# Decode attention: scores of a whole head over 512 keys on 64 partitions, K turned in place in halves

## The chip, the core and the metric

The kernel runs on one core of one Trainium2 chip. The metric is the device time of one launch in microseconds, lower is better. Engines: PE (matmul), DVE (vector), ACT (scalar), POOL (GpSimd, only used for a few memsets), SP (issues every DMA).

## What is computed

Four layers act on one token `x` of width 640: attention (A), mixer (B), A, B, both times with the same weights and caches. Each A takes 32 heads of width 192 over the last 4096 keys of the caches:

```python
W = min(4096, max(256, Sk // 4))                      # 4096
q = (x @ wq).reshape(B, Sq, Hq, Dh)                   # 32 heads x 192
k = k_cache[:, :, Sk - W:, :]; v = v_cache[:, :, Sk - W:, :]
scores = jnp.einsum("bhqd,bhkd->bhqk", q, k) * (Dh ** -0.5)
p = _softmax(scores, axis=-1)
o = jnp.einsum("bhqk,bhkd->bhqd", p, v)
return o.transpose(...).reshape(B, Sq, Hq * Dh) @ wo
```

The mixer B is a small chain of layer norms, a gelu and two matrices (640x1536 and 1536x640); it is not touched here. K and V of one head are 1.5 MB each in bf16, so nearly all the work is reading the caches: 32 heads, K and V, twice.

## The kernel before

**Cells.** SBUF holds 12 cells of 128 x 6144 bf16 (`NCELL`), each big enough for K or V of one head (partition p has keys 32p to 32p+31). `take` (L146) gets the cell that was freed longest ago, `give` (L152) frees one. `layer_stream` (L247) fixes the order of all loads: in each group of four heads it alternates K of the next group with V of the running one, then wo. `need` (L291) issues the loads in this order, and SP issues each as soon as the last reader of its cell is done. At most eight loads are under way: each waits for the landing of the eighth before it.

**Kept heads.** Layer 0 takes the groups from the last to the first, layer 1 from the first to the last. K of heads 0 to 7 (`NKEEP`), which are the last two groups of layer 0 and the first two of layer 1, stay in SBUF in turned form and aren't read again in layer 1. V of head 3, and V of head 2 and a part of V of head 4 in several places, stay as well. At the end of layer 0 the kept K hold eight cells, and four go round for the last loads: V 4 to 7 make room for V 0 to 3, two blocks of wo, w3 and w4.

**Turning K.** TensorE needs K with the head's width on partitions. `transpose_quart` (L433) has DVE turn blocks of 32x32 words, a quarter of a head per instruction (128x768 uint32, L450). A kept head's quarters go into a cell of their own (`take(("T", h))`). All others go through the four quarters of one cell, the area (`area`, L430). K's cell is freed when its last quarter is turned (`give(("k", layer, h))`, L452).

**Scores.** `scores` (L524) multiplies the query blocks (16 columns of weights, `Qblk`) with turned K. Each quarter of K has its own 32 partitions of PSUM, that is its own column group of the array: six matmuls of 256 keys per quarter, 24 per head. A call with two quarters alternates between two column groups, a call with four (kept heads in layer 1) between four. The scores of four heads gather on 128 partitions x 256 in one half of `ST_both`, one PSUM bank; `next_scores` (L544) takes the halves in turn.

**Softmax of a group.** `softmax_steps` (L551) returns seven steps: `part_max` (DVE, maximum per partition, L557), `turn_max` (PE, L562), `full_max` (DVE, L567 and L572), `spread_max` (PE, L580; ACT copies the bias, L583, and does exp with its sum, L586), `turn_p` (DVE, L591 and L593), `swap` (PE, 16 matmuls, L605; ACT, L608; PE sums, L613) and `recip` (DVE, L620 and L622).

**The order.** It is written out by hand in `attention` (L726), and each engine does its instructions in this order. `T(h, half)` turns two quarters, `S(h, half, ...)` scores them. For each group the loop at L819 first does the softmax of the running group around `T` and `S` of the next group's first head (L857 to L897), together with the query projection and the output projection of the group before. Then, for each running head, come PV (`pv`, L645: 16 matmuls of PT and V, L654, then DVE drains O with L661), `T` and `S` of the next group's next head, and `o_fold` (L663) of the running one. In layer 1 the first half of the next K is turned ahead of PV's drain (L913). The last group but one (`hurry`) scores its last two heads after PV of its second and third head (L941 to L953), and starts the last softmax there. In layer 1 that group has an order of its own (`quick`).

Of the kernel before, what the change touches and what calls it, by code (L numbers as in the profile page):

```python
# [18 lines left out]
P = 128  # L19
# [40 lines left out]
def kernel(  # L60
# [31 lines left out]
    NT = 4  # L92
    QUART = NFB * (NGK // NT) * P * 2
    FREE = NT * QUART
# [57 lines left out]
    def give(key):  # L152
        free.append(cell_of.pop(key))
# [276 lines left out]
    area = [None, 0]  # L430
    SW = P * NGK // NT

    def transpose_quart(layer, h, q):  # L433

        if layer == 1 and h < NKEEP:
            return kept[h][:, q * QUART:(q + 1) * QUART]
        Kn = need("k", layer, h)
        NY = NFB * (NGK // NT)
        Ku = Kn[:].bitcast(U32).rearrange("p (j y b) -> p j y b", j=NJ4, b=32)
        if layer == 0 and h < NKEEP:  # L440
            if q == 0:
                kept[h] = take(("T", h))
            T = kept[h][:, q * QUART:(q + 1) * QUART]
        else:
            if area[0] is None:
                area[0] = take(("area", layer))
            T = area[0][:, area[1] * QUART:(area[1] + 1) * QUART]
            area[1] = (area[1] + 1) % NT
        Tu = T.bitcast(U32).rearrange("p (y j b) -> p j y b", y=NY, j=NJ4)
        nc.vector.transpose(Tu, Ku[:, :, q * NY:(q + 1) * NY])  # L450
        if q == NT - 1:
            give(("k", layer, h))  # L452
        return T

    def qproj_steps(c, xc, part=None, row=None):
# [29 lines left out]
        def spread():  # L485
# [7 lines left out]
            Xq = o_bytes[:, 2 * (SW + 2 * QH):][:, 0:4 * n].rearrange("p (t b) -> p t b", b=4)  # L493
# [30 lines left out]
    def scores(h, Ts, q0, ST_ps, hq):  # L524
# [3 lines left out]
        views = [T.rearrange("p (g f i t) -> p g f i t", f=NFB, g=ng, i=P) for T in Ts]  # L528
        for f in range(NFB):
            for t in range(2):  # L530
                n = 2 * f + t
                for i, T4 in enumerate(views):
                    r = 32 * (q0 + i)
                    nc.tensor.matmul(  # L534
                        ST_ps[r:r + QW, :].rearrange("p (g i) -> p g i", g=ng), lhsT=Q[n],
                        rhs=T4[:, :, f, :, t],
# [3 lines left out]
    ST_both = psS.tile([P, 2 * SW], F32, name="ST_ps")  # L540
# [3 lines left out]
    def next_scores():  # L544
        turn[0] += 1
        i = turn[0] % 2
        return ST_both[:, i * SW:(i + 1) * SW]
# [3 lines left out]
    def softmax_steps(n, ST_ps, sc, space, bank=None):  # L551
        held = {}
        halves = space.bitcast(BF16)

        def part_max():
            pm = short("pm")
            nc.vector.tensor_reduce(out=pm[:], in_=ST_ps, op=ALU.max, axis=AX.X)  # L557
# [560 lines left out]
```

## Time and profile before

| | |
|---|---|
| median of 3 runs | 511.87 us (511.39 to 512.92) |
| the profiled execution | 511.54 us, of which the span is 509.7 us |
| busy: PE, DVE, ACT, POOL | 313.2, 292.6, 48.9, 3.7 us |
| mean granted TensorE clock | 0.723 |
| DMA | 214.63 MB, 421 GB/s |
| turning K (L450) | x224, 946 ns each, 201.6 us |
| scores (L534) | x1536, 157.8 us busy |
| PV (L654) | x1000 recorded, 90.2 us busy |

How to read it: one execution is shown, in us from the start of the span. PE's matmuls overlap one another, so their busy time is less than their number times their mean. A releaser is what an engine waited for last. The time to landing of a DMA issue counts from the issue by SP to its last byte, so it holds the wait behind the loads that were issued before. The granted clock is a share of full speed, in windows of 3.41 us.

### The profile page before, as it was taken

To read this page: it belongs to the slowest core of one execution; us is meant where nothing else is said; L and a number is where in the kernel's file an instruction comes from. 1 tells how busy PE (TensorE), PEld (TensorE's weight loads), DVE (VectorE), ACT (ScalarE), POOL (GpSimd) and SP (SyncE) were. 2 spreads that over 40 slices of the span, in tenths; PEclk is the share of its full clock that TensorE was granted. 3 is DMA by queue.
4 is the path that set the end of the run, shared out by engine and by line. 5 is a ranking of instruction groups with operands and counts; after the bars stand their busy time and mean duration, and the time that the engine had idled before them with its cause. 6 is when DMAs were issued, how large, how long until landed. Compare 5 with 4: busy or idle time off the path is not lost.

```text
span 509.7 us, 9498 instructions
## 1 busy us (share of the span) xinstructions
PE 313.2 (61%) x4084; PEld 186.2 (37%) x4084; DVE 292.6 (57%) x604; ACT 48.9 (10%) x173; POOL 3.7 (1%) x16
## 2 busy tenths in 40 slices
PE   1056667666565555857655766767655765557685
PEld 0023333343332322534333643544322433324354
DVE  2067557666674755566723244968666656656522
ACT  1000101010010100001010101010100101001101
POOL 2000000000000000000000000000000000000000
PEclk9999756777597766576765586789887766857655
DMA  8999999999999999999999999999999999999996
GB/s 370 432 432 429 430 441 432 429 429 422 417 426 441 432 425 446 432 402 458 429 391 413 381 438 424 439 429 429 426 429 433 429 430 432 418 437 429 418 409 250
DMA packets 12014, 214.63 MB, mean 421 GB/s; under 512 B 2564, under 2 KB 3076, under 8 KB 7428
## 3 DMA queue, kind: packets, MB, share of 16 engines
q1 hardware_dynamic: 11972, 214.02, 98.5%
q8 instruction: 32, 0.52, 0.4%
q14 instruction: 10, 0.08, 0.0%
HBM read 214.01 MB, written 0.00 MB: 420 GB/s over the span
## 4 chain that ended last, share of the span: by engine, by line
DMA 60%; PE 20%; DVE 14%; issue 4%; ACT 1%; SPq 1%; DVEq 0%; ACTq 0%
DMA cell<-in_A_k_cache_dram 37%; DMA cell<-in_A_v_cache_dram 19%; DVE cell L450 9%; PE ST_ps L534 9%; PE O_ps L654 5%; DMA cell<-in_B_w_dram 4%; DVE o_sb L661 2%; PE qT_ps L480 1%; PE y_ps L1062 1%; PE nb_ps L580 1%; DVE words L557 1%; PE l_ps L613 1%; DVE V_ps L643 1%; DVE o_sb L591 1%; SPq L55 0%
## 5 line engine op out<-in xcount | busy, mean ns | idle before, releaser
L534 PE MATMUL ST_ps<-cell,Qblk 128*16 128x256 bf16 x1536 | 157.8, 364 | 110.8 <-DVE cell L450 66.6
L450 DVE STREAM_TRANSPOSE cell<-cell 128x768 uint32<-128x768 uint32 x224 | 201.6, 946 | 33.7 <-DMA cell<-in_A_k_cache_dram 31.6
L534 PEld LDWEIGHTS <-Qblk 128*16 128x16 bf16 x1536 | 84.7, 108 | 175.1 <-issue 150.2
L654 PE MATMUL O_ps<-cell,PT 128*2 128x384 bf16 x1000 | 90.2, 436 | 11.0 <-DMA cell<-in_A_v_cache_dram 9.1
L661 DVE STREAM_TRANSPOSE o_sb<-O_ps 128x384 f32<-128x384 f32 x64 | 36.7, 573 | 79.6 <-PE O_ps L654 79.5
L654 PEld LDWEIGHTS <-PT 128*2 128x2 bf16 x1024 | 41.2, 96 | 26.9 <-issue 18.7
L669 ACT ACTIVATE words<-oT_ps,words 32x6 bf16<-32x6 f32 x40 | 10.3, 257 | 163.6 <-PE oT_ps L668 150.3
L591 DVE STREAM_TRANSPOSE o_sb<-o_sb 128x256 bf16<-128x256 bf16 x15 | 6.7, 445 | 31.9 <-ACT o_sb L586 14.2
L668 PE MATMUL oT_ps<-o_sb,Lq 128*32 128x6 f32 x160 | 13.4, 192 | 10.7 <-DVE o_sb L661 10.1
L668 PEld LDWEIGHTS oT_ps<-o_sb,Lq 128*32 128x32 f32 x160 | 11.6, 137 | 20.4 <-issue 14.4
L674 ACT ACTIVATE words<-oT_ps,words 32x6 bf16<-32x6 f32 x24 | 6.2, 257 | 107.6 <-PE ST_ps L534 79.6
L480 PE MATMUL qT_ps<-words,wq_sb 128*128 128x1 bf16 x210 | 7.2, 165 | 12.9 <-DMA wq_sb<-in_A_wq_dram 12.0
L494 DVE TENSOR_TENSOR o_sb<-qT_ps,words 128x24 bf16<-128x24 f32 (+1 forms) x18 | 2.9, 163 | 20.2 <-PE qT_ps L480 17.4
L583 ACT COPY o_sb<-nb_ps 128x1 f32<-128x1 f32 x15 | 2.4, 159 | 102.2 <-PE nb_ps L580 102.2
L480 PEld LDWEIGHTS <-wq_sb 128*128 128x128 bf16 x210 | 6.8, 104 | 14.1 <-DMA wq_sb<-in_A_wq_dram 13.1
L605 PEld LDWEIGHTS <-ident 128*32 128x32 bf16 x256 | 5.8, 111 | 14.8 <-issue 14.5
L469 PE MATMUL qr_ps<-wq_sb,words 128*1 128x384 bf16 x90 | 10.7, 376 | 0.0
L700 PE MATMUL yr_ps<-cell,words 128*1 128x320 bf16 x108 | 10.4, 335 | 0.0
L673 PE MATMUL oT_ps<-o_sb,Lq 128*32 128x6 f32 x48 | 5.9, 194 | 6.8 <-DVE o_sb L672 6.8
L580 PEld LDWEIGHTS nb_ps<-words,o_sb 1*128 1x128 f32 x30 | 7.0, 287 | 7.2 <-issue 5.4
L673 PEld LDWEIGHTS oT_ps<-o_sb,Lq 128*32 128x32 f32 x48 | 5.0, 134 | 11.2 <-issue 9.1
L580 PE MATMUL nb_ps<-words,o_sb 1*128 1x1 f32 x30 | 8.2, 339 | 1.5 <-DVE o_sb L572 1.5
(159 smaller groups left out, 200.3 us busy)
## 6 DMA issues: line engine op xcount, KB each, us to landing
cell<-in_A_k_cache_dram SPq DMA_DIRECT2D x56, 1536.0 KB, 27.7
cell<-in_A_v_cache_dram SPq DMA_DIRECT2D x56, 1536.0 KB, 27.7
cell<-in_A_wo_dram SPq DMA_DIRECT2D x13, 960.0 KB, 27.5
wq_sb<-in_A_wq_dram SPq DMA_DIRECT2D x5, 1536.0 KB, 13.4
cell<-in_A_v_cache_dram SPq DMA_DIRECT2D x6, 768.0 KB, 23.7
cell<-in_B_w_dram SPq DMA_DIRECT2D x1, 1536.0 KB, 11.8
cell<-in_B_w_dram SPq DMA_DIRECT2D x2, 768.0 KB, 10.3
cell<-in_A_wo_dram SPq DMA_DIRECT2D x3, 480.0 KB, 17.0
```

The source lines that it names most:

```text
L450: nc.vector.transpose(Tu, Ku[:, :, q * NY:(q + 1) * NY])
L469: nc.tensor.matmul(qr_ps[32 * i:32 * i + 1, :], lhsT=xc[:, kc:kc + 1], rhs=wq_sb[:, kc, t0 * P + i * N:t0 * P + (i + 1) * N], start=(kc == ...
L480: nc.tensor.matmul(qT_ps[:, tl:tl + 1], lhsT=wq_sb[:, kc, t * P:(t + 1) * P], rhs=xc[:, kc:kc + 1], start=(kc == 0), stop=(kc == ND - 1))
L534: nc.tensor.matmul(ST_ps[r:r + QW, :].rearrange("p (g i) -> p g i", g=ng), lhsT=Q[n], rhs=T4[:, :, f, :, t], start=(hq == 0 and n == 0), s ...
L580: nc.tensor.matmul(nb_ps[:], lhsT=held["w"], rhs=one[0:1, :], start=True, stop=True)
L591: nc.vector.transpose(held["PrT"], held["Pr"])
L654: nc.tensor.matmul(O_ps[r:r + 2, :], lhsT=PT[:, hq, 2 * i:2 * i + 2], rhs=v_pair(V, h, 2 * i * Dh, 2 * Dh), start=(i < 4), stop=(i >= NB - 4))
L661: nc.vector.transpose(o_sb[:], O_ps.rearrange("p (e a c) -> p e c a", e=2, c=NA))
L668: nc.tensor.matmul(oT_ps[r, :], lhsT=Lq[:], rhs=o_sb[:, e, :, e], start=(e == 0), stop=(e == 1))
L669: nc.scalar.activation(oT[r, :], oT_ps[r, :], ACTF.Copy, scale=rl[r, 0:1])
L673: nc.tensor.matmul(oT_ps[r, :], lhsT=Lq[:], rhs=o2, start=True, stop=True)
L700: nc.tensor.matmul(yr_ps[32 * i:32 * i + 1, :], lhsT=oT[:, k:k + 1], rhs=wo_t[:, k * D + i * N:k * D + (i + 1) * N], start=(k == 0), stop= ...
```

## The change

- K is turned in two halves of 128x1536 words instead of four quarters, and in place: `transpose_half` writes into the cell it reads. There is no area, and no second cell for a kept head. K's cell is freed after the head's scores instead of after its last turn.
- `scores` runs once per head, after both halves are turned: 12 matmuls over 512 keys, alternating between two column groups. The scores of a group lie on 64 partitions x 512. The groups use partitions 0 to 63 and 64 to 127 of the same PSUM bank in turn.
- The softmax steps work on 64 partitions x 512; `swap` has 8 matmuls instead of 16.
- `spread_max` of the running group comes ahead of the scores of the next group's first head.
- In both layers, for the second and third head of a group (not in the last group but one), both halves of the next K are turned ahead of PV's drain.

```diff
-    NT = 4
-    QUART = NFB * (NGK // NT) * P * 2
-    FREE = NT * QUART
+    NT = 2
+    HP = P // 2
+    HALF = NFB * (NGK // NT) * P * 2
+    FREE = NT * HALF
...
+    def transpose_half(layer, h, q):
         if layer == 1 and h < NKEEP:
+            return kept[h]
         Kn = need("k", layer, h)
         NY = NFB * (NGK // NT)
+        Ku = Kn[:].bitcast(U32).rearrange("p (j y b) -> p j y b", j=NJ4, b=32)[:, :, q * NY:(q + 1) * NY]
+        nc.vector.transpose(Ku, Ku)
+        if q == NT - 1 and layer == 0 and h < NKEEP:
+            kept[h] = Kn
+            cell_of["T", h] = cell_of.pop(("k", 0, h))
+        return Kn
...
+    def scores(h, K, ST, hq):
...
+        T = K.rearrange("p (j g f i t) -> p g j f i t", j=NJ4, g=NGK, f=NFB, t=2)
         for f in range(NFB):
             for t in range(2):
                 n = 2 * f + t
+                for i in range(NT):
+                    r = ST[0] + 32 * i
                     nc.tensor.matmul(
+                        ST_both[r:r + QW, :].rearrange("p (g j i) -> p g j i", g=ng, j=NJ4), lhsT=Q[n],
+                        rhs=T[:, ng * i:ng * (i + 1), :, f, :, t],
                         start=(hq == 0 and n == 0), stop=(hq == QH - 1 and n == NCOL - 1))
-    ST_both = psS.tile([P, 2 * SW], F32, name="ST_ps")
+    ST_both = psS.tile([P, SW], F32, name="ST_ps")
...
     def next_scores():
         turn[0] += 1
-        i = turn[0] % 2
-        return ST_both[:, i * SW:(i + 1) * SW]
+        i = turn[0] % 2 * HP
+        return i, ST_both[i:i + HP, :]
...
+        def S(h, half, ST, hq):
+            if half == 0:
                 return
+            K, _ = Th.pop((h, 0)), Th.pop((h, 1))
+            scores(h, K, ST, hq)
+            if h >= NKEEP:
+                give(("k", layer, h))
+            elif layer == 1:
+                give(("T", h))
...
                     T(h0, 0)
                     part_max()
                     T(h0, 1)
-                    S(h0, 0, ST_n, 0)
                     turn_max()
                     full_max()
+                    spread_max()
                     S(h0, 1, ST_n, 0)
-                    spread_max()
...
-                elif layer == 1 and nxt and 0 < hq < 3:
+                elif nxt and not hurry and 0 < hq < 3:
                     T(nxt[0][1], 0)
+                    T(nxt[0][1], 1)
                 pv(layer, h, hq, PT, steps[3] if quick and hq == 3 else fold)
```

In `softmax_steps` every slice of 128 partitions becomes the 64 of the group, `PrT` goes to the other 64, and the columns of the scratch move to fit.

## The prediction

> **What bounds the kernel now.** I read the page's slices, DMA queues and chain of waits, then the DMA issues in short windows, the chain from 240 to 292 us, and the timeline there.
>
> ```profile
> DMA  8999999999999999999999999999999999999996
> ...
> q1 hardware_dynamic: 11972, 214.02, 98.5%
> ...
> DMA 60%; PE 20%; DVE 14%; issue 4%; ACT 1%; SPq 1%; DVEq 0%; ACTq 0%
> ```
>
> The 16 DMA engines are busy 98.5% of the span, at about 430 GB/s in most slices. The change alters no load: the same 214 MB come in the same order and pieces. So a quicker PE or DVE gains nothing by itself. The change can gain what idle DMA time there is, or lose time where a load is issued too late. A load is issued when its cell is released, so the question is which releases move, and how full the queue is there. The last column of these issues (windows 130-160, 240-262, 262-270 and 289-290 us) is the time to landing:
>
> ```profile
> cell<-in_A_k_cache_dram SPq DMA_DIRECT2D x3, 1536.0 KB, 27.7
> ...
> cell<-in_A_v_cache_dram SPq DMA_DIRECT2D x4, 1536.0 KB, 11.6
> ...
> cell<-in_A_v_cache_dram SPq DMA_DIRECT2D x1, 960.0 KB, 7.0
> ...
> cell<-in_A_k_cache_dram SPq DMA_DIRECT2D x1, 1536.0 KB, 8.8
> ```
>
> 27.7 us means some seven loads of 3.65 us stand ahead (1.57 MB at 430 GB/s): there a release may come 15 us later for nothing. 7.0 and 8.8 us are what a nearly empty queue gives: there each us of delay is a us of idle DMA. Two places are so thin: the last V loads of layer 0, when eight cells hold kept K, and the first K of layer 1. The chain passes through both:
>
> ```profile
> 244.66 11.95 DMA cell<-in_A_v_cache_dram
> ...
> 256.65 0.85 PE O_ps L654 x16
> ...
> 259.38 0.57 PE nb_ps L580 x2
> ...
> 260.16 0.66 ACT o_sb L586 x2
> ...
> 262.31 1.41 PE O_ps L654 x14
> 263.74 7.02 DMA cell<-in_A_v_cache_dram
> ...
> 288.00 1.46 PE ST_ps L534 x23
> ```
>
> At 263.74 the load of V 2 starts the moment PV of head 0 has freed its cell, and 7.02 us later its landing ends the next wait. After 288.00 the scores of head 0 free the cell of the first K of layer 1 (issued at 289.50). How far the compute lags just before, in the timeline:
>
> ```profile
> 245.74 7.18 DVE L450 STREAM_TRANSPOSE cell<-cell 128x768 uint32<-128x768 uint32 x8 [0.49 <-DMA cell<-in_A_k_cache_dram]
> ...
> 253.01 0.82 PE L654 MATMUL O_ps<-cell,PT 128*2 128x384 bf16 x16 [0.80 <-DMA cell<-in_A_v_cache_dram]
> ...
> 256.65 0.82 PE L654 MATMUL O_ps<-cell,PT 128*2 128x384 bf16 x16 [1.04 <-DMA cell<-in_A_v_cache_dram]
> ```
>
> Each step waits for its load, but by 0.49, 0.80 and 1.04 us only: more than 1 us of extra work on this path shows.
>
> **The parts, priced.**
>
> *K turned in halves, in place.* 224 turns of 0.946 us (128x768) become 112 of 128x1536. Bounds: 1.89 us (two old ones) and 1.6 (512 elements take 0.69 to 0.73 us at L643, so about 0.23 per 256 more). I take 1.75, near the upper row. The gain of 0.1 us per half is on DVE, covered by loads almost everywhere.
>
> *No area.* One cell more, until head 11 is scored in layer 0 and from head 8 on in layer 1; kept K no longer needs two cells while it turns. By the load order the K and V loads up to 250 us are issued earlier. In return a plain K is freed after its scores, 3 to 5 us later; with 27.7 us to landing that is hidden. But the last V loads of layer 0 circulate through four cells in both kernels, with the same releasers from V 1 on (PV of 6, 7, 0). So the extra cell doesn't help at the thin place: 0.
>
> *Scores of a whole head.* 24 matmuls of 256 columns become 12 of 512 on two column groups. The rows:
>
> ```profile
> 139.25 1.50 PE L534 MATMUL ST_ps<-cell,Qblk 128*16 128x256 bf16 x12
> ...
> 288.00 1.46 PE L534 MATMUL ST_ps<-cell,Qblk 128*16 128x256 bf16 x24 [0.28 <-DVE Qblk L518]
> ```
>
> Two groups give 12 in 1.50 us; a kept head, on four groups, gives 24 in 1.46. Both are at granted clock 0.50. Twelve of 512 columns on two groups are two such dozens: bounds 1.46 and 3.0; I take 2.85 at clock 0.5, and 1.5 at clock 1.0 (eleven take 0.84 there). For a plain head it is the same PE work, no longer begun behind the second half's turn; for a kept head 1.4 us more.
>
> *Softmax on 64 partitions x 512.* Twice the elements per lane: maximum 0.39 to at most 0.78, take 0.62; exp 0.56 to at most 1.13, take 0.80; turning P 0.445 to at most 0.89, take 0.70 (384 f32 take 0.573). The small 1x128 steps halve (-0.1), as do the 16 matmuls of L605 (-0.05).
>
> *spread_max ahead of S, and a new wait.* The first score matmul of each next group carries a wait for ScalarE, which the old one had not: it stands behind exp of the running group. Queued behind it on PE are the projections, P's swap and PV.
>
> *Next K ahead of O.* K of the next head is turned during PV, before O is drained: about 2 us less for two heads in each group, but not in the last but one (`hurry`), which is the thin place.
>
> **The sum at the thin place,** from 231.35, where both kernels start on K 0 behind the drain of O 11 (the +3 us that this order costs at the head of the group before is given back by its two early turns). The second half of K 0 ends at 235.35, exp at 237.7 (238.0 before). Scores of K 0, hidden until 236.6 before, now run 237.7-240.55. Projection 0.96, then P's swap, cast and sums: PV of 4 starts at 242.9 (239.99, +2.9). Scores of 1 need 2.85 (2.05): PV of 5 at 247.4 (243.3), its drain ends at 249.1, so K 2 starts there (245.74, +3.35). It ends at 252.6, its scores at 255.4, PV of 6 at 256.7. K 3 is ready by 256.1. Its scores take 1.45 to 2.85, I say 2.3, to 259.0; maximum, turn and fold 1.4: PV of 7 at 260.5 (256.65, +3.8). Softmax adds 0.24 + 0.25 - 0.15 = 0.35. V 2 is issued at 267.9 instead of 263.74. About 0.2 us of queue is left there: **+4.0 us** of idle DMA. V 1, issued 2.8 later, has 12.3 us to landing and stays above 8.8; wo, 4.1 later, falls from 10.9 to 6.8, just the 7.0.
>
> The first K of layer 1 waits for the scores of head 0: 2.85 instead of 1.46, **+1.4 us**. The next seven kept heads put PV about 6 us later, but V and wo loads wait in a filling queue; the K issued at 321.09 has 13.3 us to landing, and 13.3 - 5.9 + 1.4 = 8.8 just holds: 0, up to 1.5. The tail: softmax and scores of the last group +2.0 us, against waits for DMA of 0.34, 0.60, 0.29 and 0.94 us from 494 to 503: 0, up to 0.5. Idle DMA elsewhere: 0.
>
> Sum: 511.54 (the profiled run; span 509.7) + 4.0 + 1.4 = **517.0**, 1.0% over the median of 511.87, which is 0.33 above the profiled run.
>
> **Rivals.**
>
> *The clock comes up (20%).* The scores run at clock 1.0 in 244-258 us and the lag stays in the waits of 0.49 to 1.04: V 2 late by 0.5 only, plus 1.4 for the first K: 513.4, between 512 and 514.8. For: PE is denser here. Against: granted clock 0.50 in 234.31-241.14 though PE was busy 3.41 of 3.41 us in the first of these windows. The Trainium skill (TensorE: Matmul & The Clock Gate, Part 1) says the clock is full after a window of 3.4 us in which PE was busy. The trace agrees at 247.96-251.38 (2.67 us busy, then 1.00) and not at 234.31-237.72 (3.41 busy, then 0.50).
>
> *The lag compounds (20%).* All scores and PVs at clock 0.5, K 3 too, and the K at 321 falls behind: V 2 late by 7, first K 1.4, later 1.5: 521.4. For: the clock is 0.5 in most of 200-245. Against: three windows at 0.94 to 1.00 between 244 and 258.
>
> *The change gives room (8%; the other side).* The freed cell and the earlier turns keep the queue full through the layer's end. Price: at 280-296 us the DMA moves 365, 404, 396 and 351 GB/s instead of 430, so (65 + 26 + 34 + 79) x 4 us = 0.82 MB, 1.9 us at most, to 509.6. It decides only if V 2 and the first K are issued no later than now. Against: their releasers are the same, and each has more work ahead of it.
>
> *It doesn't do what it says:* the two column groups are to let the next head be scored while the last group is read, but the wait for exp stands in between. This is in my sum; if only part of exp is waited for, 0.8 us less.
>
> **How the numbers follow.** My forecast, 514.8 to 519.5, has 52%; the rivals 20, 20 and 8%. The range 512.8 to 522.0 takes in most of both neighbours. About 0.3% (1.5 us) is what a measurement of this kernel can tell from no change. Of the first rival about half falls within it, of the third a half, the rest being faster: faster 4%, within 14%, slower 82%.
>
> **What would show it.** L450's successor x112 at 1.75 us; score matmuls x768, a head 2.85 us at clock 0.5; the V load near 264 issued 4 us later with about 7 us to landing, DMA slices thinner near 264-272 and 289-294 and full elsewhere. Wrong, if V 2 is issued within 1 us of 263.74, if DMA shows holes before 250 us (then late K releases matter), or if the loss lies after 310 us.

## The result and the profile after

| | before | after |
|---|---|---|
| median of 20 runs | 511.57 us (510.93 to 512.92) | 513.41 us (512.25 to 515.55) |
| ratio of the two | 1 | 1.0041, 95% interval 1.0031 to 1.0052 |
| profiled execution (span) | 511.54 (509.7) us | 513.0 (511.2) us |
| DMA moved | 214.63 MB | 214.50 MB |
| mean granted clock | 0.723 | 0.716 |

The changed kernel is slower by 1.84 us in the medians, 0.41% by the ratio. The forecast was 517.0: the sign is right, 513.41 lies in the range from 512.8 to 522.0, but the loss is a third of the one forecast, and outside the likeliest case's own range (514.8 to 519.5).

The page of the changed kernel, with the slices, the DMA queue, the chain, and the groups that were repriced (calls, busy us and mean ns, idle time before them and its releaser):

```profile
DMA  9999999999999999999989999999999999999995
...
q1 hardware_dynamic: 11972, 214.02, 98.3%
...
DMA 23%; DVE 3%; PE 3%; issue 2%; ACT 1%; SPq 0%; ACTq 0%
...
L441 DVE STREAM_TRANSPOSE cell<-cell 128x1536 uint32<-128x1536 uint32 x112 | 194.6, 1758 | 32.3 <-DMA cell<-in_A_k_cache_dram 31.7
L526 PE MATMUL ST_ps<-cell,Qblk 128*16 128x512 bf16 x768 | 152.6, 512 | 68.8 <-DVE cell L441 53.2
...
L585 DVE STREAM_TRANSPOSE o_sb<-o_sb 64x512 bf16<-64x512 bf16 x15 | 10.6, 706 | 23.9 <-ACT o_sb L579 23.9
```

The bound is the same: DMA busy for 98.3% of the span, the same bytes from the caches, no thin slice before 255 us. The chain's shares add up to a third only, because here it can be followed back no further than 348.50 us. It says nothing of the two thin places, so these must be read from the issues and the timeline.

The same four windows of DMA issues as before (the third and fourth are the thin places, the fourth widened to 293 us); the last column is the time to landing:

```profile
cell<-in_A_k_cache_dram SPq DMA_DIRECT2D x4, 1536.0 KB, 27.7
...
cell<-in_A_v_cache_dram SPq DMA_DIRECT2D x3, 1536.0 KB, 13.6
...
cell<-in_A_v_cache_dram SPq DMA_DIRECT2D x1, 960.0 KB, 5.9
...
cell<-in_A_k_cache_dram SPq DMA_DIRECT2D x1, 1536.0 KB, 8.6
```

27.7 us again: a full queue in the middle of layer 0, though K is freed later. 13.6 for 11.6: the V loads of the layer's end are issued into a fuller queue. At V 2 it is 5.9 for 7.0: this load finds less ahead of it than before.

The timeline of the changed kernel through both thin places:

```profile
237.85 2.73 PE L526 MATMUL ST_ps<-cell,Qblk 128*16 128x512 bf16 x12 [1.14 <-ACT o_sb L579]
...
248.78 6.71 DVE L441 STREAM_TRANSPOSE cell<-cell 128x1536 uint32<-128x1536 uint32 x4
250.57 0.39 PE L526 MATMUL ST_ps<-cell,Qblk 128*16 128x512 bf16 x1 [2.36 <-DVE cell L441]
...
255.75 1.63 PE L526 MATMUL ST_ps<-cell,Qblk 128*16 128x512 bf16 x12
...
265.55 2.04 SPq L182 DMA_DIRECT2D cell<-in_A_v_cache_dram  x4
...
288.60 2.73 PE L526 MATMUL ST_ps<-cell,Qblk 128*16 128x512 bf16 x12 [0.28 <-DVE Qblk L510]
...
291.37 0.33 SPq L157 DMA_DIRECT2D cell<-in_A_k_cache_dram  x1
```

V 2 is issued at 265.55 (263.74 before), the first K of layer 1 at 291.37 (289.50). With the times to landing above, V 2 lands 0.7 us later, so 1.1 of its 1.8 us are taken up by the queue; the first K lands 1.7 us later, so only 0.2 of its 1.9 us are. Three more issues stand behind the scores of the next kept heads: before at 291.01, 292.55 and 294.17, after at 293.71, 295.48 and 297.78. So the second place is four issues late by 1.9, 2.7, 2.9 and 3.6 us, not one.

What that does to the DMA is seen in the view of windows: PE, PEld, DVE, ACT and POOL busy (instructions), granted clock, DMA share and GB/s. First before, then after:

```profile
265.00:270.00 5.00, 2.32 (x22) 1.17 (x22) 0.67 (x2) 0.45 (x2) 0.00 (x0) 0.50 0.94 383
270.00:288.00 18.00, 11.04 (x228) 7.99 (x228) 7.44 (x37) 2.77 (x13) 0.00 (x0) 0.50 1.01 403
288.00:298.00 10.00, 8.92 (x216) 6.10 (x220) 3.42 (x12) 0.47 (x2) 0.00 (x0) 0.80 1.04 414
298.00:310.00 12.00, 7.77 (x126) 4.34 (x116) 4.02 (x14) 1.60 (x6) 0.00 (x0) 0.72 0.98 421
```

```profile
265.00:270.00 5.00, 3.86 (x64) 2.51 (x57) 1.41 (x5) 0.52 (x2) 0.00 (x0) 0.50 0.80 294
270.00:288.00 18.00, 10.73 (x221) 7.76 (x221) 7.11 (x34) 2.77 (x13) 0.00 (x0) 0.50 1.02 413
288.00:298.00 10.00, 9.59 (x94) 3.73 (x91) 1.16 (x9) 0.46 (x2) 0.00 (x0) 0.75 0.90 337
298.00:310.00 12.00, 9.29 (x108) 4.45 (x108) 5.42 (x17) 1.28 (x4) 0.00 (x0) 0.86 1.07 454
```

Two holes: (383 - 294) x 5 = 445 KB in 265 to 270, and (414 - 337) x 10 = 770 KB in 288 to 298, which at 430 GB/s are 1.0 and 1.8 us. Behind each the queue fills and a part comes back: 10 x 18 = 180 KB and 33 x 12 = 396 KB, 0.4 and 0.9 us. That leaves 1.5 us, as much as the two spans differ by (511.2 - 509.7). The agreement is partly luck. Counted from the start, the changed kernel has moved 0.14 MB more than the kernel before by 265 us (112.95 against 112.81 MB), 0.50 MB less by 310 us (130.60 against 131.10) and 0.39 MB less by 480 us (203.70 against 204.09), which is 0.9 us; the other 0.6 us arise after that (experiment 7 comes back to it). The theory that was tested is: the loss is made at these two places, by late releases, and nowhere else. The rivals are the late K releases in layer 0, the wait for exp, the clock, and the end of the kernel.

### The profile page after: what moved, and what is told of

Read it like the earlier page. It is cut to its first block, busy times and chain, and to the rows that moved or that the text cites. A ratio compares the mean times of both kernels' runs of the same rounds, so it can differ in the third digit from the quotient of the medians.

```text
span 511.2 us, 7558 instructions
## 1 busy us (share of the span) xinstructions
PE 295.9 (58%) x3188; PEld 145.2 (28%) x3188; DVE 297.4 (58%) x492; ACT 52.1 (10%) x173; POOL 3.7 (1%) x16
## 2 busy tenths in 40 slices
DMA packets 12005, 214.50 MB, mean 420 GB/s; under 512 B 2564, under 2 KB 3076, under 8 KB 7428
## 3 DMA queue, kind: packets, MB, share of 16 engines
q1 hardware_dynamic: 11972, 214.02, 98.3%
## 5 line engine op out<-in xcount | busy, mean ns | idle before, releaser
L441 DVE STREAM_TRANSPOSE cell<-cell 128x1536 uint32<-128x1536 uint32 x112 | 194.6, 1758 | 32.3 <-DMA cell<-in_A_k_cache_dram 31.7
L526 PE MATMUL ST_ps<-cell,Qblk 128*16 128x512 bf16 x768 | 152.6, 512 | 68.8 <-DVE cell L441 53.2
L648 PE MATMUL O_ps<-cell,PT 128*2 128x384 bf16 x1000 | 99.0, 430 | 6.6 <-DMA cell<-in_A_v_cache_dram 4.7
L526 PEld LDWEIGHTS <-Qblk 128*16 128x16 bf16 x768 | 46.3, 105 | 144.1 <-issue 121.8
L585 DVE STREAM_TRANSPOSE o_sb<-o_sb 64x512 bf16<-64x512 bf16 x15 | 10.6, 706 | 23.9 <-ACT o_sb L579 23.9
L573 PE MATMUL nb_ps<-words,o_sb 1*64 1x1 f32 x30 | 4.9, 230 | 26.7 <-DVE o_sb L565 26.7
L662 PE MATMUL oT_ps<-o_sb,Lq 128*32 128x6 f32 x160 | 13.1, 190 | 11.3 <-DVE o_sb L655 10.8
L662 PEld LDWEIGHTS oT_ps<-o_sb,Lq 128*32 128x32 f32 x160 | 11.8, 135 | 23.6 <-issue 18.3
L472 PE MATMUL qT_ps<-words,wq_sb 128*128 128x1 bf16 x210 | 7.1, 165 | 13.1 <-DMA wq_sb<-in_A_wq_dram 12.2
L552 DVE TENSOR_REDUCE words<-ST_ps 64x1 f32<-64x512 f32 x16 | 10.8, 674 | 4.3 <-PE ST_ps L526 4.2
L573 PEld LDWEIGHTS nb_ps<-words,o_sb 1*64 1x64 f32 x30 | 4.0, 190 | 29.2 <-issue 27.7
L579 ACT ACTIVATE o_sb<-ST_ps,o_sb,words 64x512 bf16<-64x512 f32 x15 | 11.6, 773 | 0.5
L472 PEld LDWEIGHTS <-wq_sb 128*128 128x128 bf16 x210 | 6.7, 102 | 16.2 <-DMA wq_sb<-in_A_wq_dram 13.3
## 6 DMA issues: line engine op xcount, KB each, us to landing
cell<-in_A_k_cache_dram SPq DMA_DIRECT2D x56, 1536.0 KB, 27.6
cell<-in_A_v_cache_dram SPq DMA_DIRECT2D x56, 1536.0 KB, 27.7
cell<-in_A_wo_dram SPq DMA_DIRECT2D x13, 960.0 KB, 27.7
wq_sb<-in_A_wq_dram SPq DMA_DIRECT2D x5, 1536.0 KB, 13.6
```

The source lines that it names most:

```text
L441: nc.vector.transpose(Ku, Ku)
L472: nc.tensor.matmul(qT_ps[:, tl:tl + 1], lhsT=wq_sb[:, kc, t * P:(t + 1) * P], rhs=xc[:, kc:kc + 1], start=(kc == 0), stop=(kc == ND - 1))
L526: nc.tensor.matmul(ST_both[r:r + QW, :].rearrange("p (g j i) -> p g j i", g=ng, j=NJ4), lhsT=Q[n], rhs=T[:, ng * i:ng * (i + 1), :, f, :, ...
L552: nc.vector.tensor_reduce(out=pm[S, :], in_=ST_ps, op=ALU.max, axis=AX.X)
L573: nc.tensor.matmul(nb_ps[S, :], lhsT=held["w"], rhs=one[0:1, :], start=True, stop=True)
L579: nc.scalar.activation(out=Pr, in_=ST_ps, func=ACTF.Exp, bias=nb_sb[:, 0:1], scale=sc[S, 0:1], accum_out=lpart[:, 0:1])
```

## The experiments

All ratios are against the kernel before, timed on the same chip in the same job, with 95% intervals; a ratio is not the quotient of the two medians, and the two can differ by some tenths of a us. Issue times are those of the profiled executions.

**1. What the K turned ahead is worth.** In the changed kernel the new early turn is taken back, so the kernel before's half turn in layer 1 remains:

```diff
-                elif nxt and not hurry and 0 < hq < 3:
+                elif layer == 1 and nxt and 0 < hq < 3:
                     T(nxt[0][1], 0)
-                    T(nxt[0][1], 1)
```

> Kernel after without the turning of the next K ahead of O (the line of the kernel before: only in layer 1, and only the first half). Theory of two gaps: those turns lie where the load queue is 3 to 25 us deep, and the last group but one of layer 0 is not touched by the line, so nothing moves at the two places: 513.4 within 0.3. Rival, turning a whole K (3.5 us) ahead of O holds up the drain of O on DVE and with it the release of V cells: without it the time falls by 0.5 us or more.

543.36 us, ratio 1.0620 (1.0606 to 1.0633): all theories missed by 30 us. Its page and its timeline in 100 to 131 us:

```profile
DMA  9999999999999999995659999999999999999980
...
cell<-in_A_k_cache_dram SPq DMA_DIRECT2D x56, 1536.0 KB, 17.4
```

```profile
103.61 0.58 DVE L655 STREAM_TRANSPOSE o_sb<-O_ps 128x384 f32<-128x384 f32 x1 [4.04 <-PE O_ps L648]
...
105.90 0.59 PE L526 MATMUL ST_ps<-cell,Qblk 128*16 128x512 bf16 x1 [2.33 <-DVE cell L441]
...
111.55 0.58 DVE L655 STREAM_TRANSPOSE o_sb<-O_ps 128x384 f32<-128x384 f32 x1 [3.99 <-PE O_ps L648]
```

The DMA is still full at 104 us, but a head now takes 7.94 us from one drain to the next (103.61 to 111.55), and its two loads 7.3. DVE waits 4 us for PV, and PE then waits 2.33 us for the turn, in a ring: nothing of one head's turn lies beside the next PV. Each head falls 0.6 us behind, the queue empties (17.4 us to landing for a K in place of 27.6), and from 240 us on the DMA has holes. In the last slice of the page it moves 3 GB/s where the changed kernel moves 233, so a part of the loss lies at the end. So in this order a whole-head score is only affordable with the turn ahead. The other way round, the same early turn in the kernel before:

```diff
-                elif layer == 1 and nxt and 0 < hq < 3:
+                elif nxt and not hurry and 0 < hq < 3:
                     T(nxt[0][1], 0)
+                    T(nxt[0][1], 1)
```

> Kernel before with one part of the change alone: the K of the next head is turned whole ahead of O in both layers, into the area as before. By the ledger of loads the queue of before is 20 us deep up to 190 us and 5 to 10 us at 220 to 260 us; turning earlier frees K cells earlier and makes it deeper there, which moves no landing; the last group but one of layer 0 is not touched. Theory of two gaps: 511.6 within 0.3. Rival, the turns ahead of O alone change the time (a later drain of O, or an earlier release of cells at the thin places): off by more than 0.5.

511.45, ratio 0.9997 (0.9988 to 1.0005): nothing. With the early turn the late K releases cost nothing either: the DMA of the changed kernel is full to 265 us.

**2. K 3 earlier at the first place.** In the layer's last group but one, K of the third next head is turned ahead of PV's drain. In the first kernel K of the fourth is also turned whole and scored ahead of the third PV, in the second its scores stay behind that PV (the edit of the second):

```diff
+                elif hurry and hq == 1:
+                    T(nxt[0][1], 0)
+                    T(nxt[0][1], 1)
                 elif nxt and not hurry and 0 < hq < 3:
...
                     T(h3, 0)
-                    S(h3, 0, ST_n, q3)
                     T(h3, 1)
                 elif hurry and hq == 2:
```

> Kernel after; in the last group but one of layer 0 the K of head 2 is turned ahead of the PV of head 5, and the K of head 3 is turned and scored ahead of the PV of head 6 instead of behind it. Theory of two gaps: the change costs 1.8 us because the load queue runs dry at two places, at 265 to 267.5 us (V 2 of layer 0 issued at 265.55 instead of 263.74) and at 291 to 293 us (first K of layer 1 issued at 291.37 instead of 289.50, of which 0.65 is handed on from the first place). Then V 2 is issued 1.5 to 2.5 us earlier, the idle time of the first place (some 0.85 us) closes, and the time falls by 0.6 to 0.9 us, to about 512.7 (ratio to before 1.0022). Rival, the cost lies in the order of every group (turns ahead of O, the exp wait) and not at this place: 513.4, as after.

> Kernel after; as in a_early the K of head 2 of layer 0 is turned ahead of the PV of head 5 and the K of head 3 in one piece behind the scores of head 2, but the scores of head 3 stay behind the PV of head 6, which then fits between the two score runs (V 6 lands at 251.5, the scores of head 2 should end at about 251.9). Theory of two gaps: V 2 is issued at about 264.2 instead of 265.55, the load queue no longer runs dry at the first place, and the time falls by 0.6 to 0.9 us to about 512.6 (ratio about 1.002). Rival, the lag at the first place is not what costs: 513.4.

515.08 (ratio 1.0066, 1.0052 to 1.0081) and 514.23 (1.0045, 1.0033 to 1.0057): both miss the 512.6 to 512.7 that was expected; the first is worse than the changed kernel, the second no better. V 2 was issued at 266.73 and 266.05. The reason stands in the two timelines, the first kernel's and then the second's:

```profile
252.94 2.72 PE L526 MATMUL ST_ps<-cell,Qblk 128*16 128x512 bf16 x11 [1.05 <-DVE cell L441]
```

```profile
254.13 2.77 PE L526 MATMUL ST_ps<-cell,Qblk 128*16 128x512 bf16 x12
```

In the first, PV of 6 stands behind scores that wait for a turn, and starts at 255.46 (254.75 in the changed kernel, 253.01 in the kernel before). In the second it starts at 252.90, but the scores that follow take 2.77 us at clock 0.5, and PV of 7 comes at 257.98, behind them and behind the maximum's transposition, which waits for DVE. The direction agrees with the theory: with V 2 later than 265.55 by 1.2 and 0.5 us, the medians are higher than the changed kernel's by 1.7 and 0.8 us. By the ratios only the first of the two differences stands out (1.0066 and 1.0045 for 1.0041).

**3. The lag put into the kernel before.** Matmuls of zero weights into the scores' sums: 16 ahead of the second half of head 3 in layer 0, and in the second kernel also 20 behind the scores of head 0 in layer 1:

```diff
+        Zb = Qblk[:, h // QH % 2, NM:NM + 1].broadcast_to([P, QW])
+        for k in range(more):
+            nc.tensor.matmul(ST_ps[r:r + QW, :]..., lhsT=Zb,
+                rhs=views[i][:, :, k // len(views) % NFB, :, 0], start=False, stop=False)
```

> Kernel before; 16 more matmuls of 128x256 with a zero stationary operand on two column groups are put ahead of the second half of the scores of head 3 in layer 0 (they add zero). By the 12 of 128x512 of the kernel after (2.73 us) they take about 1.8 us, the lag that V 2 has in the kernel after. Theory of two gaps: V 2 is issued at about 265.5, its first data comes some 0.4 to 0.7 us later than in before (2.90 us of queue less the 1.45 us that an empty queue takes leave 1.45 us of slack), and the run takes 0.4 to 0.7 us longer: 512.0 to 512.3. Rival, a lag here is swallowed and the cost comes from elsewhere: 511.6. The step of the prediction (slack of 0.2 us, then one for one): 513.2.

> Kernel before with the 16 zero matmuls ahead of the second half of the scores of head 3 in layer 0, and 20 more of 128x256 on four column groups behind the scores of head 0 in layer 1 (24 take 1.46 us, so some 1.2 us): the two lags of the kernel after, and nothing else of the change. Theory of two gaps: first K of layer 1 issued 1.8 to 1.9 us later, landing 1.2 later, time 512.8 to 513.3, nearly all of what the change costs. Rival, at least half of the cost lies elsewhere (tail, exp wait, turns ahead of O): at most 512.4.

511.66 (1.0001, 0.9992 to 1.0009) and 512.25 (1.0017, 1.0004 to 1.0031). The first tells little: its 16 matmuls took 1.07 us and went into the 1.04 us that PV of 7 had waited for its load; V 2 was issued at 263.49, no later. It does show that a lag as small as these waits costs nothing. In the second, V 2 went out at 264.63 and the first K at 290.59, 0.9 and 1.1 us late. That is half of the lags that were meant, and the time misses the theory's 512.8 to 513.3 and lies in the rival's range (at most 512.4); with half the lags it decides neither.

**4. The wait for exp, and the clock.** In the changed kernel, first `spread_max` goes back behind the scores; second, four idle matmuls (128x512) keep PE busy while it waits for w4 at 282 us:

```diff
-                    spread_max()
                     S(h0, 1, ST_n, 0)
+                    spread_max()
```

```diff
+        if layer == 0:
+            warm = psm.tile([32, 512], F32, tag="psm")
+            for i in range(4):
+                nc.tensor.matmul(warm[:], lhsT=Eq[:, 0, :], rhs=wq_sb[:, 0, 0:512], start=(i == 0), stop=(i == 3))
         w4 = need("w4", layer)
```

> Kernel after with the scores of head h0 of each group put back ahead of the exp (they then need not wait for ACT, 1.14 us in the profile, but the exp comes behind 2.7 us of scores). Theory of two gaps: the exp and the turn of P move by about 2 us, the turn of K 1 with them, and in the last group but one of layer 0 this hands some 1.2 us on to V 2 (issued at about 266.7): 514 to 515. Rival, the wait for the exp is what the change costs: 512.3 to 512.6.

> Kernel after with four matmuls of 128x512 into a spare bank while TensorE waits for w4 at the end of layer 0 (282.6 to 284.4 us); they feed nothing. If the granted clock comes up by them, the scores of head 0 in layer 1 (2.73 us at a granted clock of 0.5, about 1.6 at 1.0) release the cell of the first K about 1.1 us earlier, at 290.3 instead of 291.37. Theory of two gaps: then the time falls by 0.4 to 0.8 us to about 512.8. Rival, the second place does not count because the queue makes it up later: 513.4. If the clock stays at 0.5 the run tells nothing of the places: 513.4.

513.22 (1.0033, 1.0021 to 1.0045) and 513.49 (1.0037, 1.0024 to 1.0051): neither can be told from the changed kernel. The wait of 1.14 us for exp is real, and worth nothing that could be measured. (V 2 went out at 264.64 in this kernel, not at the 266.7 that was expected.) The second is inconclusive: the idle matmuls ran (281.85 to 283.74), but the clock stayed at 0.50 to 292.7 us and the scores of head 0 took 2.73 us as before. So what a faster clock would be worth there was not seen this way. One thing more came out of it: up to 281 us this kernel is the changed one, and it issued V 2 at 264.39, not 265.55. Single profiles of one order differ by about 1 us there.

**5. Delays that are sure to arrive.** Since the first lag of experiment 3 was swallowed, four idle matmuls of 128x512 (some 1.9 us) were put into the kernel before, right ahead of PV of head 0 in layer 0, right ahead of the scores of head 0 in layer 1 (three of 128x400 in the first kernel), or both:

```diff
                     early = steps[5](), steps[6]()
+                    if layer == 0:
+                        spare = psm.tile([32, 512], F32, tag="psm")
+                        for i in range(4):
+                            nc.tensor.matmul(spare[:], lhsT=Eq[:, 0, :], rhs=wq_sb[:, 0, 0:512], start=True, stop=True)
...
         qb[1]()
+        if layer == 1:
+            ...
         ST = next_scores()
```

> Kernel before with TensorE held up at the two places and nothing else of the change: four matmuls of 128x512 into a spare bank ahead of the PV of head 0 in layer 0 (1.89 us, measured in a_warm) and three of 128x400 ahead of the scores of head 0 in layer 1 (some 1.2 us). They feed nothing. V 2 should be issued 1.9 us later (263.74 to 265.6) and the first K of layer 1 some 1.8 us later (289.50 to 291.3), the two lags of the kernel after. Theory of two gaps: 512.8 to 513.4, all or nearly all of the 1.84 us. Rival, at least half of the cost lies elsewhere: at most 512.4.

> Kernel before with only the four spare matmuls ahead of the PV of head 0 in layer 0 (1.89 us). Theory of two gaps: 1.45 us of the delay go into the load queue's slack (its first data came 2.90 us after the issue, 1.45 when the queue was empty), 0.4 to 0.8 us show: 512.0 to 512.4. The prediction's slack of 0.2 us and one for one: 513.3. Rival, a delay here is swallowed: 511.6.

> Kernel before with only four spare matmuls ahead of the scores of head 0 in layer 1 (1.9 us). Theory of two gaps: the first K of layer 1 is issued at 291.4; 2.78 us lie between its issue and first data in before and 1.4 to 1.8 when the queue is empty, so 1.0 to 1.4 us go into slack and 0.5 to 0.9 show: 512.1 to 512.5. Rival, swallowed: 511.6. Rival, every later K release of layer 1 is late too and adds up: over 513.

| | V 2 issued | first K issued | median (before) | ratio |
|---|---|---|---|---|
| changed kernel | 265.55 | 291.37 | 513.41 (511.57) | 1.0041 (1.0031 to 1.0052) |
| both delays | 265.67 | 291.95 | 514.07 (511.63) | 1.0036 (1.0020 to 1.0053) |
| first only | 265.71 | 290.61 | 512.80 (511.63) | 1.0020 (1.0011 to 1.0030) |
| second only | 263.55 | 291.97 | 512.54 (511.63) | 1.0015 (1.0007 to 1.0024) |

The kernel with both delays, in the same windows:

```profile
265.00:270.00 5.00, 2.94 (x58) 1.90 (x57) 1.39 (x5) 0.52 (x2) 0.00 (x0) 0.84 0.82 306
...
288.00:298.00 10.00, 9.24 (x216) 6.22 (x219) 2.10 (x13) 0.77 (x4) 0.00 (x0) 0.74 0.85 325
```

Delays of about the changed kernel's size at its two places (V 2 late by 1.9 us for its 1.8, the first K by 2.5 for its 1.9), with nothing else of the change, give two holes like its own (306 and 325 GB/s for 294 and 337) and a loss like its own (2.4 us for 1.84 by the medians, 1.0036 for 1.0041 by the ratios). That such lags are enough is shown. Delayed alone, the first place costs 1.2 us and the second 0.9, which add up to 2.1 for the 2.4 of both. The first was expected at 0.4 to 0.8 us, by 1.45 us of slack in front of V 2: a miss, with more of the delay showing than the count of slack gave. The first hands part of its lag to the second: with V 2 late by 1.97, the first K was late by 1.1 although nothing was added there.

**6. The places repaired in the changed kernel.** For the first, the second kernel of experiment 2, and the maximum's transposition (`turn_max`) moved behind PV of 7, so that this PV waits only for PE:

```diff
                     steps = softmax_steps(len(cur), ST_n, sc, o_words)
                     steps[0]()
-                    steps[1]()
...
-                    for step in steps[4 if quick else 2:5]:
+                    for step in steps[4 if quick else 1:5]:
```

> Kernel after with the order of a_early2 and the transposition of the maxima of the last group of layer 0 behind the PV of head 7 instead of ahead of it. In before that PV waits for the data of V 7 (it starts at 256.65); in after it starts at 257.2 to 258.4 behind the scores of head 3, their maximum and its transposition. Theory of two gaps: the PV of head 7 starts at about 256.7 to 257, V 2 is issued at about 263.9, the first gap is that of before, and the time falls by 0.4 to 0.9 us against after: 512.5 to 513.0. Rival, the first place does not matter: 513.4.

> Kernel of a_fix1 once more, beside the two others on the same chip: 512.9 by its first runs, 513.2 to 513.4 if these were lucky (a_fix12, of the same first place, took 513.2).

In the first run V 2 is issued as in the kernel before, at 263.83, in the second at 264.73; the first K at 290.75 and 290.85. 512.92 and 512.84 against 511.63 and 511.46, ratios 1.0015 (1.0005 to 1.0025) and 1.0027 (1.0016 to 1.0039): by the medians some 0.5 us of the 1.84 are gone, but only the first interval lies clear of the changed kernel's (1.0031 to 1.0052). The rest must come from the second place or elsewhere. Two more edits were tried there: the second part of the query projection moved behind the scores of head 0 in layer 1, and the softmax words kept apart so that exp runs during PV of 7:

```diff
         qa[0]()
-        qb[0]()
+        if layer == 0:
+            qb[0]()
...
-        qb[1]()
+        if layer == 0:
+            qb[1]()
...
                 if (hq, half) == (0, layer):
+                    if layer == 1:
+                        qb[0]()
+                        qb[1]()
                     qb[2]()
```

> Kernel of a_fix1; in layer 1 the projection of q for the second half of the first group's heads (15 matmuls, some 0.47 us) is put behind the scores of head 0 instead of ahead of them. In a_fix1 V 2 is issued at 263.83 as in before, but the first K of layer 1 still at 290.75 instead of 289.50, because the scores of head 0 take 2.73 us instead of 1.46. Theory of two gaps: the first K is issued at about 290.2 and the time falls by 0.2 to 0.5 us against a_fix1, to 512.3 to 512.7. Rival, what a_fix1 still costs lies behind the two places (late last pieces of w4): 512.9, as a_fix1.

> Kernel of a_fix12, and the softmax of layer 0's last group gets words of its own (in the room of w3, which is loaded later), so that the maxima and the exp need not wait for the drain of the PV of head 7. V 2 should be issued at about 262.8, 0.9 us ahead of before. Theory of two gaps: the queue then has slack at the first place, and at most 0.3 us more are gained: 512.0 to 512.6. Rival: the earlier V 2 moves the whole end of layer 0 and with it the first K of layer 1 forward: below 511.8.

> Kernel before with the same two edits (own words for the softmax of layer 0's last group; scores of head 0 of layer 1 ahead of the second half's projection). Theory of two gaps: before itself loses little there (idle DMA of 1.14 us between 260 and 310), the first K of layer 1 is issued at about 289.0: 511.1 to 511.6. Rival, no gap of before is set by these chains: 511.6.

513.20 (1.0039, 1.0026 to 1.0051) and 513.23 (1.0034, 1.0021 to 1.0046): no gain over the first repair, and none over the changed kernel either, although V 2 goes out at 263.71 and 263.13 in them, as early as in the kernel before; and in the kernel before 511.80 (1.0008, 0.9999 to 1.0017), no gain either. The timeline of the first of them shows why (L472 is the moved part):

```profile
287.88 2.73 PE L526 MATMUL ST_ps<-cell,Qblk 128*16 128x512 bf16 x12 [0.28 <-DVE Qblk L510]
290.54 0.56 PE L472 MATMUL qT_ps<-words,wq_sb 128*128 128x1 bf16 x15
```

The scores of head 0 began at 287.88, against 287.98 in the kernel with the first repair: the 15 matmuls had lain beside DVE's work on the queries and cost nothing there. Behind the scores of head 0 they delay those of head 1 (291.46 against 290.77).

**7. The second place shortened.** The remaining suspect is the scores of the kept heads themselves, 2.73 us for 1.46 at clock 0.5. So half of the score matmuls of heads 0 to 3 in layer 1 were left out, in the changed kernel and in the repaired one; such a kernel lacks half of these heads' products and serves only to measure. A head then has the 1.45 us at clock 0.5 that the kernel before has there:

```diff
                 n = 2 * f + t
+                if n >= NC:
+                    continue
...
-            scores(h, K, ST, hq)
+            scores(h, K, ST, hq, NCOL // 2 if layer == 1 and h < QH else NCOL)
```

> Kernel after with the same half of the scores of heads 0 to 3 of layer 1 left out, and the first place as in after. Theory of two gaps: the second place's own share goes, the first's stays (0.7 to 0.95 us in the ledger of loads): 512.2 to 512.8. Rival, the second place has no cost of its own: 513.4.

> Kernel of a_fix1, but in layer 1 the scores of heads 0 to 3 leave out the last three of their six column blocks (half of the products of those heads), so that each run of scores takes about 1.4 us at a granted clock of 0.5, as the whole head takes in before (1.46). Both places then have the times of before. Theory of two gaps: the first K of layer 1 is issued at about 289.4, and the time is that of before within 0.4 us: 511.3 to 512.0. Rival, 0.8 us of the cost lies behind the two places: 512.9, as a_fix1.

512.20 (before 511.46; 1.0012, 1.0002 to 1.0022) and 512.11 (1.0009, 1.0000 to 1.0018). The first of them, in the same windows:

```profile
265.00:270.00 5.00, 3.81 (x64) 2.48 (x57) 1.41 (x5) 0.52 (x2) 0.00 (x0) 0.50 0.81 295
...
288.00:298.00 10.00, 9.42 (x105) 4.01 (x104) 2.84 (x13) 0.46 (x2) 0.00 (x0) 0.80 1.06 422
```

The first hole is as deep as in the changed kernel (295 for 294 GB/s), the second is gone (422 for 337), and the loss falls from 1.84 to 0.74 us by the medians: **the second place takes about 1.1 us**, and the intervals of the two ratios lie apart.

The first place's share is not settled by the times. Its repair gained some 0.5 us in experiment 6, nothing measurable together with the further edits there, and here 0.1 us (512.20 to 512.11), where it was not whole either (V 2 at 264.11, first K at 290.07, against 263.74 and 289.50). In bytes the first place is there: from 265 to 288 us the changed kernel falls behind the kernel before by 0.25 MB (0.6 us), from 288 to 310 us by another 0.39 MB (0.9 us).

With both treated, 0.65 us of the medians stay, at an interval of the ratio that begins at 1.0000. The profiles show that a loss can also arise at neither place. Packets and MB of the loads' queue from 0 to 480 us, in the kernel before, the changed kernel, the second kernel here, and the second kernel of experiment 3:

```profile
q1 hardware_dynamic: 9351, 204.09, 99.5%
...
q1 hardware_dynamic: 9339, 203.70, 99.4%
...
q1 hardware_dynamic: 9355, 204.19, 99.7%
...
q1 hardware_dynamic: 9352, 204.09, 99.6%
```

By 480 us the last two have moved as many bytes as the kernel before, or more, and yet their executions are 1.0 and 2.0 us longer (spans 510.7 and 511.7 for 509.7). In all four the span ends 3.5 us after the last load's last packet, so the computing behind that load is not what is longer: the last loads come late. In the changed kernel this is 0.6 of the 1.5 us between the two spans. No experiment isolates it, and the kernel of experiment 3 is the kernel before with nothing changed at its end. So the two places are shown, but "nowhere else" is not; the end of the kernel stays untested as a third.

No version beat the kernel before, so there is none to recommend.

## Why the prediction was partly right and where it failed

- **The bound, and two thin places:** right. Loads unchanged, the DMA full elsewhere, the loss at V 2 and at the first K of layer 1. Experiment 5 makes the loss from these two alone, and experiment 7 removes one hole by one place's edit. The 0.6 us behind 480 us are in neither.
- **K in place, freed late: 0.** Right for this kernel, but the reason given (27.7 us to landing hides it) is only half of it. Experiment 1 shows that 27.7 holds only while a head takes less than its two loads; without the turn ahead it takes 7.94 us against 7.3, and the kernel is 31.7 us slower than the kernel before. The turn ahead was priced as "about 2 us less for two heads in each group", a side matter; it is what makes the rest possible.
- **The prices of the pieces:** right. Forecast and measured: half a turn 1.75 and 1.758, a head's scores 2.85 and 2.73 at clock 0.5 and 1.5 and 1.53 at clock 1.0, the maximum 0.62 and 0.674, exp 0.80 and 0.773, turning P 0.70 and 0.706.
- **The wait for exp:** it is there (1.14 us), and its removal in experiment 4 brought nothing measurable.
- **The sum at the thin place: "V 2 is issued at 267.9", 4.2 us late; it was 1.8.** The first half of the working held: scores of K 0 at 237.7 (237.85), PV of 4 at 242.9 (242.75), K 2 from 249.1 (248.78). Then it drifted by 2.1 us up to PV of 7 (260.5 forecast, 258.39 measured), in small pieces: the turn of K 2 ended 0.4 us earlier, the scores of 2 (eleven of twelve from 252.23) and PV of 6 (from 254.75) overlapped on PE and took 0.6 us less, the scores of 3 took 1.63 us from 255.75 where 2.3 us to 259.0 had been forecast, and the maximum and its transposition 0.4 us less.
- **The step that failed: "About 0.2 us of queue is left there: +4.0 us of idle DMA".** This was two errors: the lag was 1.8 us and not 4.2, and the slack was not 0.2. V 2 landed only 0.7 us later, so the queue took up 1.1 us. The 128 packets of V 2's first load (7,680 bytes each) show it: the middle one began 3.88 us after the issue in the kernel before and 2.73 in the changed one. I had taken 7.0 us to landing, a nearly empty queue, for an empty one. The 2.90 and 1.45 us that the expectations call the first data are a count, the time by which as many bytes had moved as were issued ahead of V 2; its very first packets began at 1.06 and 0.97 us. A slack of 1.45 us taken from that count is too large, as 0.2 was too small. Of the +4.0 us of idle DMA a hole of 1.0 us was found, of which 0.4 came back.
- **The first K, +1.4 us:** near. It was issued 1.87 us later, of which 1.27 came from its own scores and 0.6 was handed on by the first place, and it landed 1.7 us later: here the lag shows almost one for one, as forecast. The prediction looked for the next kept heads' lag only in the K at 321 us; three issues directly behind the first K are late by up to 3.6 us. These make the second hole the deeper one, where the prediction had it at a quarter of the sum.
- **The two were added.** That holds within the noise: delayed alone they cost 1.2 and 0.9 us, together 2.4 (ratios 1.0020, 1.0015 and 1.0036). What the sum left out is that the queue fills behind each hole and gives part of it back (0.4 and 0.9 us above), and that the second place inherits part of the first's lag.
- **The K at 321 us "just holds":** it was issued at 326.62 and landed 9.3 us later, so it held. **The tail, 0 to 0.5:** its computing costs nothing: the last PV still waits for its load (0.46 us at 495.93, 0.34 before), and the span ends 3.5 us after the last load packet in both kernels. But 0.6 us of late loads behind 480 us were in no term of the sum.
- **The rivals.** "The clock comes up" gave 513.4, which is the number measured, and the stated range holds 513.41 because it was drawn to take in most of this rival. That the number agrees is luck. Its mechanism was a part of the truth only: the scores of 3 ran at a higher clock (1.63 us), but V 2 was late by 1.8 us and not by 0.5 (0.65 to 1.8 in three profiles of the same order), and most of the difference is slack and overlap. "The lag compounds" did not occur. "Room" is there but small: by 265 us the changed kernel has moved 0.14 MB more than the kernel before, 0.3 us, and then it loses more than that.

## What to carry to other kernels

Where the DMA is the bound, do not price a late release by the time to landing alone. Count the bytes that are issued and not yet moved when the load goes out, and check the price with a delay, because the count was a rough guide too: V 2 was 1.8 us late with 1.45 us counted ahead of it and landed 0.7 later, and the first K was 1.9 us late with 1.0 to 1.4 counted and landed 1.7 later. List every issue that stands behind the lengthened step, not the first alone. Before delays along two engines are added up, write down when each step may start, since steps overlap and the clock changes between them (here 2.1 us up to PV of 7). Compare the bytes moved since the start at several points, which shows a loss that lies outside the windows one has chosen. To prove a place, put in a delay well above the waits that are already there (here 1.9 us against 0.5 to 1.0), and see in the trace that it arrived.

## What the runs showed of the hardware that was not expected

- **An instruction fetch and the time at which a load is seen as complete go together.** In 11 profiles of the changed kernel and its variants (all but the one of experiment 1), the first turn of K 0 in layer 0 begins either at 231.2 to 231.5 or at 229.5 to 229.9 us. All six of the first kind have a 16 KB packet on the instruction queue at 229.1 to 229.4; in the five of the second it comes at 236.6 to 238.4. The instruction queue in 229 to 231.5 us and the turn in the changed kernel, and then the turn in the second kernel of experiment 4, where that queue has no packet in this stretch:

```profile
q8 instruction: 1, 0.02, 2.6%
...
231.41 1.78 DVE L441 STREAM_TRANSPOSE cell<-cell 128x1536 uint32<-128x1536 uint32 x1 [4.00 <-DMA cell<-in_A_k_cache_dram]
```

```profile
229.54 1.78 DVE L441 STREAM_TRANSPOSE cell<-cell 128x1536 uint32<-128x1536 uint32 x1 [2.27 <-DMA cell<-in_A_k_cache_dram]
```

  The packet itself took 1.03 us. This is a coincidence in 11 of 11 profiles, which no experiment isolates. It does not account for all of the spread at V 2: the two executions of the first repair (V 2 at 263.83 and 264.73) are both of the second kind. The Trainium skill (Runtime: NRT & Kernel Launch, Instruction fetch mechanics) says that instructions are fetched in 16 KiB blocks through a DMA queue of the sequencer's own, and that this is hidden; the size agrees. That a fetch delays the loads beside it is not shown by any run here beyond this coincidence.
- **A busy PE does not always bring the clock.** In the kernel before PE was busy for 3.41 of 3.41 us in the granted window from 233.92 to 237.33, and the next window stayed at 0.50; in the window from 247.57 it was busy for 2.88 us, and the next was at 1.00. In the second kernel of experiment 4 the windows from 279.08 and 282.49 had 3.18 and 3.15 us of busy PE, and the clock stayed at 0.50 to 292.7 us; neither of these was quite full.
- **A load's landing can lie further behind its bytes late in the kernel.** Many loads are issued when the eighth before them has landed. Count the time from the moment at which all bytes up to that eighth load had moved to this issue. From 130 to 175 us it is some 1.4 us in the kernel before and 1.7 in the changed one; from 455 to 480 us it is 2.2 and 2.7, and 4.1 in the second kernel of experiment 3. The differences late in the kernel, 0.5 and 1.9 us, are about what these two executions lose behind 480 us. That was not tested, and it may be part of why the changed kernel's times are spread so widely (512.25 to 515.55).
